# An attention kernel whose TensorE order is planned when it is built: a new order rule, GpSimd for part of the shifted exp terms, and up to 22 of 64 blocks for VectorE

## Chip, cores, metric

One core of one Trainium2 chip. The metric is the device time of the kernel in microseconds, the median of several executions. The program uses one core only, so an execution counts as slow when it is over 1.5% above the fastest of the same kernel; comparisons use the others.

## The reference

Two independent attention problems (the code is shortened here) over 2048 tokens, width 512, 32 heads of 16. B is plain full attention. A is causal attention inside four segments of 512 tokens, mixed with a linear-attention memory that is carried from segment to segment.

```python
def _B_ref(x, wqkv, wo):
    qkv = (x @ wqkv).reshape(B, S, 3, H, Dh).transpose(2, 0, 3, 1, 4)
    q, k, v = qkv[0], qkv[1], qkv[2]
    scores = jnp.einsum('bhqd,bhkd->bhqk', q, k) * Dh ** (-0.5)
    p = _softmax(scores, axis=-1)
    o = jnp.einsum('bhqk,bhkd->bhqd', p, v)
    return o.transpose(0, 2, 1, 3).reshape(B, S, D) @ wo

def _A_ref(x, wq, wk, wv, wo, beta):          # cut to its core, for each segment s
    a_dot = softmax(causal(qs @ ks.T * scale)) @ vs
    a_mem = (phi(qs) @ M) / (phi(qs) @ z + 1e-6)
    o = g * a_mem + (1 - g) * a_dot           # g = sigmoid(beta)
    M += phi(ks).T @ vs;  z += phi(ks).sum()
```

The time is in the exponentials: B alone has 32 x 2048 x 2048 of them.

## The kernel before

The unit of work in B is one pair of (chunk of 512 queries, group of 4 heads): 4 heads x 16 key blocks = 64 blocks of 128 keys x 512 queries. For each block TensorE makes the scores in PSUM, one engine makes the exp, and TensorE multiplies it with the values (called PV below) into one accumulator.

Most blocks get their exp from ScalarE, two or three blocks in one instruction. VectorE takes up to 19 of the 64. Its blocks use no exp instruction but the bits of float16. Score times a constant plus a bias, rounded to int16 and read as float16, is a rough power of two. Three such terms, shifted by 0, 341 and 682 and weighted with three constants, make a good exp. The weights sit in copies of the values (VD, made by GpSimd). So a VectorE block costs one eviction from PSUM, two adds in SBUF (made for two blocks at once) and three PV matmuls instead of one.

```python
EXP_D = (0.0, 341.0, 682.0)                       # the shifts
EXP_C = (1.921875 / 16, 1.5234375 / 16, 1.2109375 / 16)   # the weights, in VD
...
E1 = [(13, 0), (14, 1), (15, 2)]                  # 16 + 3 blocks may go to VectorE
...
def dve_adds():                                   # the pair evicted before the last block
    if pd_open["add"] is not None:
        tile, n, ready, ents = pd_open["add"]
        pd_open["add"] = None
        for k in range(1, NT):
            nc.vector.tensor_scalar(tile[:, k, 0:n, :], tile[:, 0, 0:n, :], EXP_D[k], None, ALU.add)
            dve_do(dve_cost(512 * n, 0.32), ready + 120)
            for e in ents[k]:
                e["ready"] = c["dve"] + LAT
...
def dve_bank(u, j=None):                          # one block on VectorE
    ...                                           # score matmul into a d_ps bank (two of these)
    nc.vector.tensor_scalar(pd[:, 0, n, :], bank[:], EXP_B, 0.0, ALU.add, ALU.max)
    d_done(dve_do(dve_cost(512), c["t"] + LAT))
    dve_adds()
```

All instructions stand in an order fixed at build time. The program keeps clocks of what it believes each engine does (`c["t"]` for TensorE, `c["act"]`, `c["dve"]`, `c["gp"]`), with assumed costs, and a loop picks the next thing for TensorE: a tile of scores for ScalarE if its PSUM slot is free, else a batch of PV matmuls, a projection, a block for VectorE, or a zero matmul (a "filler") that is meant to keep TensorE's clock up. TensorE is given its matmuls in this order. If an operand comes later than the plan believed, the matmuls behind it are held up too: the timeline after the result shows a case, a wait of 1.47 us.

```python
MM, DR, LAT = 218.0, 125.0, 250.0
def dve_cost(n, rate=1.09): return 75.0 + rate * n
def gp_do(n, ready, rate=1.05):
    c["gp"] = max(c["gp"], ready) + 100.0 + rate * n
    return c["gp"]
...
# in the loop, after a tile of scores for ScalarE has been tried (cut):
if (rd and (even >= 3 or done or (full and len(rd) >= 4) or (blocked and max(len(x) for x in byj) > 0))
        and (u["acc"] is not None or acc_free[0] <= t + 100) and (act_soon is None or act_soon > t + 200)):
    flush(u, 16 if done else min(even, 4) if even >= 3 else 3)       # a batch of PV matmuls
    continue
```

Of the kernel before, what the change touches and what calls it, by code (L numbers as in the profile page):

```python
# [35 lines left out]
NT = 3  # L36
# [5 lines left out]
def fast_path(ctx, tc, nc, A_x, A_wq, A_wk, A_wv, A_wo, A_beta, B_x, B_wqkv, B_wo, out, flag):  # L42
# [139 lines left out]

    E1 = [(13, 0), (14, 1), (15, 2)]
    useq = [("a", 0, hg) for hg in range(HG)]
# [45 lines left out]
    def d_done(time):  # L230
        dbank[dcount[0] % DBANKS] = time
        dcount[0] += 1
# [8 lines left out]
    def pe(ns, mode, key=None):  # L241

        if c["mode"] != mode or ses["base"] + max(ses["acc"].values(), default=0) < c["t"] - 1:
            if c["mode"] != mode:
                c["t"] += DR
            c["mode"] = mode
            ses["base"], ses["acc"] = c["t"], {}
        ses["acc"][key] = ses["acc"].get(key, 0.0) + ns
        c["t"] = max(c["t"], ses["base"] + ses["acc"][key])
        work.append((c["t"], ns / MM * 512 * {"full": 1.0, "col": 0.3, "row": 0.2}[mode]))  # L250

# [345 lines left out]
    def make_vd(u):  # L597
# [11 lines left out]
        second = VP_b[:, E1[0][0], o + 2 * VW * E1[0][1]:o + 2 * VW * E1[0][1] + VW]  # L609
        second = bass.AP(second.tensor, second.offset, [rows, [step, len(E1)], [1, VW]])  # L610
        for k in range(NT):
            mul = lambda dst, src: nc.gpsimd.tensor_scalar(dst, src, EXP_C[k], 1.0, ALU.mult, ALU.mult)  # L612
            mul(t[:, k, 0:NSB * VW].rearrange("p (i r w) -> p i r w", i=4, r=4), heads_of(0, [[4 * ROW, 4], [step, 4]]))
            mul(t[:, k, NSB * VW:(NSB + len(E1)) * VW].rearrange("p (r w) -> p r w", w=VW), second)
        nc.gpsimd.memset(t[:, :, NSL * VW:], 1.0)
        for k in range(NT):
            gp_do(288, max(v_ready.values()))
            gp_do(100, 0)
        VD_t[u["i"]] = t
# [38 lines left out]
    def act_tile_a(u):  # L658
# [16 lines left out]
        else:  # L675
            n = sum(512 - P * kbl for _, parts in banks for kbl, _ in parts)
            nc.scalar.activation(pT[:].rearrange("p b n -> p (b n)")[:, 0:n],  # L677
                                 pt[:].rearrange("p b n -> p (b n)")[:, 0:n], ACT.Exp, scale=0.25)
        sfree[sl] = act_do(act_cost(n), c["t"] + LAT)

        b = 0
        while b < len(banks):
            e = b + 1
            while e < len(banks) and (banks[e][1][0][0] == 3) == (banks[b][1][0][0] == 3):
# [4 lines left out]
                                    pattern=[[0, e - b], [0, w // P], [1, P]], channel_multiplier=-1)  # L689
            gp_do((e - b) * w, sfree[sl] + LAT)  # L690
            b = e
# [31 lines left out]
    def act_tile_b(u, n, but=None):  # L723
# [10 lines left out]
        nc.scalar.activation(pT[:, 0:n, :], pt[:, 0:n, :], ACT.Exp, scale=1.0 / (LOG2E * 1024.0))  # L734
        sfree[sl] = act_do(act_cost(512 * n), c["t"] + LAT)
        cnt = dict(n=n, kind=pt_out[sl])
        pt_out[sl][0] += 1
        for b, (kb, j) in enumerate(banks):
            h = 8 * u["rt"] + 2 * j + u["par"]
            u["pvq"].append(dict(j=j, c0=0, lhsT=VP_b[:, kb, VW * h:VW * h + 32], rhs=pT[:, b, :],  # L740
                                 ready=sfree[sl] + LAT, cnt=cnt, v=("b", kb)))
        return [j for _, j in banks]

    pd_open = dict(tile=None, n=0, add=None)

    def dve_adds():

        if pd_open["add"] is not None:
            tile, n, ready, ents = pd_open["add"]
            pd_open["add"] = None  # L750
            for k in range(1, NT):
                nc.vector.tensor_scalar(tile[:, k, 0:n, :], tile[:, 0, 0:n, :], EXP_D[k], None, ALU.add)  # L752
                dve_do(dve_cost(512 * n, 0.32), ready + 120)
                for e in ents[k]:
                    e["ready"] = c["dve"] + LAT

# [104 lines left out]
    def by_head(u, t):  # L861
        rd = pv_ready(u, t)
        return [[e for e in rd if e["j"] == j] for j in range(4)]

    def flush(u, rounds):

# [4 lines left out]
        for r in range(rounds):  # L871
            for j in range(4):
# [10 lines left out]
                if e["cnt"]["n"] == 0:  # L883
                    e["cnt"]["kind"][0] -= 1


# [21 lines left out]
    c.update(act=t0 + 700, dve=t0 + 1400)  # L908
    sfree[0] = sfree[1] = t0 + 900
    for u in U[:2]:  # L910
        u["ready"] = t0 + 300
# [6 lines left out]
    def fill_idle(until):  # L918
# [3 lines left out]
        n = 0  # L922
        while until - c["t"] > 300 and n < 8 and busy(until - 3413) < 3100:
            if u["acc"] is None:
# [23 lines left out]
    while True:  # L948
# [69 lines left out]
        if act_now is not None:  # L1018
# [12 lines left out]
            continue  # L1031

        u = U[pvi[0]]
        byj = by_head(u, t)
# [3 lines left out]
        even = min(len(x) for x in byj)  # L1038
        if (rd and (even >= 3 or done or (full and len(rd) >= 4) or (blocked and max(len(x) for x in byj) > 0))
                and (u["acc"] is not None or acc_free[0] <= t + 100) and (act_soon is None or act_soon > t + 200)):  # L1040
            flush(u, 16 if done else min(even, 4) if even >= 3 else 3)
            continue
        if due or du is not None or ch is not None:
            if dwhen <= t + 60:
                if due or (du is None and ch is not None and ch["due"] - 20000 <= prog[0]):
                    if act_soon is None or act_soon > t + 300:
                        chores.remove(ch)
                        ch["fn"]()
                        continue
                elif du is not None and (act_soon is None or act_soon > t + 400):  # L1050
                    dve_bank(du)
# [19 lines left out]
        fill_idle(nxt)  # L1071
        c["t"] = max(c["t"], nxt)
    run_later(1e18)
# [428 lines left out]
```

## Time and profile before

| | before |
|---|---|
| median of 4 executions | 972.54 us |
| ScalarE busy | 864.9 us (89%) |
| VectorE busy | 753.5 us (77%) |
| TensorE busy (matmuls overlap) | 822.3 us (84%) |
| GpSimd busy | 373.0 us (38%) |
| ScalarE idle (span less busy) | 111.7 us |

The profiled execution before had a span of 976.6 us; busy and idle times in this document are those of the profiled execution, times and ratios those of all.

The page of the kernel before. Its first line is busy time and instruction count by engine, PEclk is TensorE's granted clock in tenths over 40 slices of the span, the line with shares is the chain of work that ended last, and the lines with L numbers are groups: busy us, mean ns of one, then idle of that engine just before them and who ended it. In the names, s_ps and d_ps are scores for ScalarE and for VectorE, pT and pD their exps (pD holds the three shifted terms), acc is the PV accumulator.

```profile
PE 822.3 (84%) x6974; PEld 255.7 (26%) x6974; DVE 753.5 (77%) x1502; ACT 864.9 (89%) x803; POOL 373.0 (38%) x768
...
PEclk9999999898998999899999999999989998989977
...
PE 32%; ACT 28%; DVE 16%; issue 14%; POOL 9%; DMA 1%; ACTq 0%; DVEq 0%; POOLq 0%
...
L734 ACT ACTIVATE pT<-s_ps 128x1536 bf16<-128x1536 f32 (+2 forms) x613 | 701.5, 1253 | 68.8 <-PE d_ps L775 38.0
L786 DVE TENSOR_SCALAR pD<-d_ps 128x512 int16<-128x512 f32 x534 | 350.1, 680 | 56.6 <-PE d_ps L775 54.4
...
L877 PE MATMUL acc<-pD,VD 128*32 128x512 f16 x1602 | 240.5, 409 | 4.2 <-DVE tT L815 4.0
L752 DVE TENSOR_SCALAR pD<-pD 128x1024 int16<-128x1024 int16 (+1 forms) x538 | 234.1, 477 | 0.3
```

ScalarE is the busiest engine, and it idles 68.8 us before its B exps. 613 exps of 1253 ns on average are 768 us, but they are busy for 701.5 us only: one starts before the one ahead has ended. The PV matmuls on VectorE's terms hardly wait (4.2 us).

Who waited for whom, of the kernel before: the engine and its line, whom it waited for, us in total, times, the longest.

```profile
ACT pT L734 <- PE d_ps L775: 38.0, 48, 3.3
ACT pT L734 <- PE s_ps L729: 26.5, 32, 6.8
...
PE d_ps L775 <- DVE pD L786: 13.0, 30, 1.1
```

ScalarE waits for score matmuls (s_ps its own, d_ps those for VectorE that were issued beside them). TensorE waits little for VectorE to free a score bank.

Two stretches of 100 us of the kernel before: busy us and count by engine (PE, PEld, DVE, ACT, POOL), then the granted clock (the last two numbers are DMA).

```profile
500.00:600.00 100.00, 86.80 (x780) 26.48 (x779) 87.48 (x178) 95.21 (x88) 32.19 (x67) 0.97 0.02 7
800.00:900.00 100.00, 82.90 (x738) 25.26 (x738) 83.01 (x168) 90.53 (x83) 34.27 (x67) 0.91 0.00 1
```

ScalarE is above 90% in both, VectorE and TensorE not far below. The chain of waits has no single owner.

### The profile page before, as it was taken

To read this page: it belongs to the slowest core of one execution; us is meant where nothing else is said; L and a number is where in the kernel's file an instruction comes from. 1 tells how busy PE (TensorE), PEld (TensorE's weight loads), DVE (VectorE), ACT (ScalarE), POOL (GpSimd) and SP (SyncE) were. 2 spreads that over 40 slices of the span, in tenths; PEclk is the share of its full clock that TensorE was granted. 3 is DMA by queue.
4 is the path that set the end of the run, shared out by engine and by line. 5 is a ranking of instruction groups with operands and counts; after the bars stand their busy time and mean duration, and the time that the engine had idled before them with its cause. 6 is when DMAs were issued, how large, how long until landed. Compare 5 with 4: busy or idle time off the path is not lost.

```text
span 976.6 us, 18041 instructions
## 1 busy us (share of the span) xinstructions
PE 822.3 (84%) x6974; PEld 255.7 (26%) x6974; DVE 753.5 (77%) x1502; ACT 864.9 (89%) x803; POOL 373.0 (38%) x768
## 2 busy tenths in 40 slices
PE   5999998888888888898888898788988878888784
PEld 2333232222222222232222222222322222222221
DVE  3454668787888788869888987987478987989774
ACT  3898979898998889899999998989999998989982
POOL 3850625233333443444443154326345421514320
PEclk9999999898998999899999999999989998989977
DMA  7011000000000000010000000000000000000001
GB/s 221 23 44 39 6 22 2 1 1 2 1 2 12 12 1 1 6 34 1 1 1 18 6 1 1 1 1 3 22 1 12 12 1 2 1 1 1 1 7 42
DMA packets 14719, 13.83 MB, mean 14 GB/s; under 512 B 2336, under 2 KB 14624, under 8 KB 14624
## 3 DMA queue, kind: packets, MB, share of 16 engines
q1 hardware_dynamic: 12864, 11.54, 3.7%
q8 instruction: 56, 0.92, 0.4%
q10 hardware_dynamic: 1632, 1.05, 0.4%
q14 instruction: 39, 0.32, 0.1%
q0 software_dynamic: 128, 0.00, 0.0%
HBM read 8.39 MB, written 4.19 MB: 13 GB/s over the span
## 4 chain that ended last, share of the span: by engine, by line
PE 32%; ACT 28%; DVE 16%; issue 14%; POOL 9%; DMA 1%; ACTq 0%; DVEq 0%; POOLq 0%
ACT pT L734 23%; PE acc L877 13%; PE s_ps L729 8%; DVE pD L786 7%; DVE pD L752 5%; ACT pT L677 4%; POOL VD L612 4%; PE d_ps L324 3%; POOL pT L688 2%; PE d_ps L327 2%; DVE tT L815 2%; PE d_ps L494 2%; PE d_ps L775 1%; PE s_ps L667 1%; DMA beta_t<-in_A_beta_dram 1%
## 5 line engine op out<-in xcount | busy, mean ns | idle before, releaser
L734 ACT ACTIVATE pT<-s_ps 128x1536 bf16<-128x1536 f32 (+2 forms) x613 | 701.5, 1253 | 68.8 <-PE d_ps L775 38.0
L786 DVE TENSOR_SCALAR pD<-d_ps 128x512 int16<-128x512 f32 x534 | 350.1, 680 | 56.6 <-PE d_ps L775 54.4
L729 PE MATMUL s_ps<-QT_b,KT_b 32*128 32x512 bf16 x1514 | 242.1, 398 | 70.2 <-ACT pT L734 62.9
L877 PE MATMUL acc<-pT,VP_b 128*32 128x512 bf16 x1514 | 268.1, 409 | 0.0
L877 PE MATMUL acc<-pD,VD 128*32 128x512 f16 x1602 | 240.5, 409 | 4.2 <-DVE tT L815 4.0
L752 DVE TENSOR_SCALAR pD<-pD 128x1024 int16<-128x1024 int16 (+1 forms) x538 | 234.1, 477 | 0.3
L688 POOL TENSOR_SCALAR_AFFINE_SELECT pT<-pT 128x512 bf16<-128x512 bf16 (+3 forms) x192 | 97.7, 525 | 288.2 <-ACT pT L677 287.9
L775 PE MATMUL d_ps<-QT_b,KT_b 32*128 32x512 bf16 x534 | 186.4, 396 | 15.1 <-DVE pD L786 13.0
L729 PEld LDWEIGHTS <-KT_b 32*128 32x128 bf16 x1514 | 70.2, 91 | 295.3 <-issue 288.9
L677 ACT ACTIVATE pT<-s_ps 128x1024 bf16<-128x1024 f32 (+1 forms) x128 | 136.7, 1169 | 10.9 <-PE s_ps L667 9.4
L877 PEld LDWEIGHTS <-VP_b 128*32 128x32 bf16 x1514 | 68.5, 98 | 76.0 <-issue 54.4
L877 PEld LDWEIGHTS <-VD 128*32 128x32 bf16 x1602 | 59.5, 98 | 96.0 <-issue 83.1
L667 PE MATMUL s_ps<-QT_a,KT_a 32*128 32x384 bf16 (+3 forms) x512 | 57.7, 303 | 24.2 <-ACT pT L677 12.2
L612 POOL TENSOR_SCALAR VD<-VP_b 128x288 bf16<-128x288 bf16 (+1 forms) x186 | 66.9, 360 | 12.2
L815 DVE STREAM_TRANSPOSE tT<-acc 128x512 f32<-128x512 f32 x64 | 45.5, 711 | 31.4 <-PE acc L877 30.7
L877 PE MATMUL acc<-pT,VP_a 128*32 128x384 bf16 (+3 forms) x512 | 49.0, 318 | 16.2 <-POOL pT L688 12.8
L836 POOL TENSOR_TENSOR tN<-tT,RA 128x256 bf16<-128x256 f32 x31 | 20.1, 650 | 77.5 <-DVE RA L818 77.4
L337 POOL TENSOR_SCALAR QT_b<-qc,mq 128x512 bf16<-128x512 bf16 x32 | 24.1, 763 | 66.2 <-DVE qc L395 66.0
L775 PEld LDWEIGHTS <-KT_b 32*128 32x128 bf16 x534 | 40.1, 91 | 9.0 <-issue 7.7
L667 PEld LDWEIGHTS <-KT_a 32*128 32x128 bf16 x512 | 20.4, 92 | 79.5 <-issue 69.2
L337 POOL TENSOR_SCALAR QT_a<-qc,mq 128x512 bf16<-128x512 bf16 x30 | 21.8, 736 | 35.6 <-DVE qc L393 35.4
L504 DVE CAST osb<-d_ps 128x512 bf16<-128x512 f32 x28 | 19.1, 685 | 12.7 <-PE d_ps L494 12.7
(109 smaller groups left out, 613.9 us busy)
## 6 DMA issues: line engine op xcount, KB each, us to landing
out_dram<-osb SPq DMA_DIRECT2D x30, 128.0 KB, 1.7
xin<-in_B_x_dram SPq DMA_DIRECT2D x16, 128.0 KB, 2.2
xin<-in_A_x_dram SPq DMA_DIRECT2D x14, 128.0 KB, 2.1
wv_a<-in_A_wv_dram SPq DMA_DIRECT2D x1, 512.0 KB, 10.4
wv_b<-in_B_wqkv_dram SPq DMA_DIRECT2D x1, 512.0 KB, 9.9
wk_b<-in_B_wqkv_dram SPq DMA_DIRECT2D x1, 512.0 KB, 9.6
wq_b<-in_B_wqkv_dram SPq DMA_DIRECT2D x1, 512.0 KB, 10.0
wo_a<-in_A_wo_dram SPq DMA_DIRECT2D x1, 512.0 KB, 9.4
```

Of the source, the lines that this page charges most:

```text
L337: nc.gpsimd.tensor_scalar(t[:, par, :], qc[:], mq[:, par:par + 1], 1.0, ALU.mult, ALU.mult)
L612: mul = lambda dst, src: nc.gpsimd.tensor_scalar(dst, src, EXP_C[k], 1.0, ALU.mult, ALU.mult)
L667: nc.tensor.matmul(pt[:, b, col:col + w], kt[32 * j:32 * j + 32, kbl * P:(kbl + 1) * P], q[32 * j:32 * j + 32, P * kbl:512], start=(r == 0 ...
L677: nc.scalar.activation(pT[:].rearrange("p b n -> p (b n)")[:, 0:n], pt[:].rearrange("p b n -> p (b n)")[:, 0:n], ACT.Exp, scale=0.25)
L688: nc.gpsimd.affine_select(out=blk, in_=blk, compare_op=ALU.is_ge, fill=0.0, base=0, pattern=[[0, e - b], [0, w // P], [1, P]], channel_mul ...
L729: nc.tensor.matmul(pt[:, b, :], KT_b[32 * j:32 * j + 32, u["rt"], kb * P:(kb + 1) * P], q[32 * j:32 * j + 32, :], start=True, stop=True, t ...
L734: nc.scalar.activation(pT[:, 0:n, :], pt[:, 0:n, :], ACT.Exp, scale=1.0 / (LOG2E * 1024.0))
L752: nc.vector.tensor_scalar(tile[:, k, 0:n, :], tile[:, 0, 0:n, :], EXP_D[k], None, ALU.add)
L775: nc.tensor.matmul(bank[:], KT_b[32 * j:32 * j + 32, u["rt"], kb * P:(kb + 1) * P], qslice(u)[32 * j:32 * j + 32, :], start=True, stop=Tru ...
L786: nc.vector.tensor_scalar(pd[:, 0, n, :], bank[:], EXP_B, 0.0, ALU.add, ALU.max)
L815: nc.vector.transpose(tT[:].rearrange("p c d -> p (c d)"), u["acc"][:])
L877: nc.tensor.matmul(u["acc"][32 * j:32 * j + 32, e["c0"]:512], e["lhsT"], e["rhs"], start=(j not in u["started"]), stop=False, tile_positio ...
```

## The change

Its intent: ScalarE limits, so give VectorE more blocks (16 + 6 of 64). To make room on VectorE, give GpSimd, 38% busy, the second add of a pair when the plan says that GpSimd is free. And cut what TensorE does between two tiles of scores to what fits into the work that ScalarE still has queued (`room`), with smaller PV batches and more fillers against a falling clock. The core of the diff (cut: the layout of VD for six extra blocks, some latencies, the same test for projections):

```diff
-    E1 = [(13, 0), (14, 1), (15, 2)]
+    E1 = [(9, 0), (10, 1), (11, 2), (13, 0), (14, 1), (15, 2)]
...
+    GPS = -500
...
             for k in range(1, NT):
-                nc.vector.tensor_scalar(tile[:, k, 0:n, :], tile[:, 0, 0:n, :], EXP_D[k], None, ALU.add)
-                dve_do(dve_cost(512 * n, 0.32), ready + 120)
+                gp = k == NT - 1 and n == 2 and c["gp"] < c["dve"] + GPS
+                (nc.gpsimd if gp else nc.vector).tensor_scalar(tile[:, k, 0:n, :], tile[:, 0, 0:n, :], EXP_D[k], None, ALU.add)
+                if gp:
+                    gp_do(512 * n, ready + LAT)
+                else:
+                    dve_do(dve_cost(512 * n, 0.32), ready + 120)
...
+        if len(u["started"]) == 4 and busy(c["t"] - 3213) < WARM2:     # in flush: fillers
+            for j in range(4):
+                nc.tensor.matmul(u["acc"][32 * j:32 * j + 32, :], zero[:, 0:32], wq_a[:, 0, :], ...)
...
+        room = 1e9
+        if au is not None and not blocked and not stalled:
+            room = max(c["act"] - LATE, act_soon or 0) - t + SLK
...
-        if (rd and (even >= 3 or done or (full and len(rd) >= 4) or ...
-            flush(u, 16 if done else min(even, 4) if even >= 3 else 3)
-            continue
+        if rd and (u["acc"] is not None or acc_free[0] <= t + 100):
+            want = most if done else even if even >= EVEN else min(3, most) if full and (len(rd) >= 4 or blocked) else 0
+            r = int(min(want, 4 if not done else 16, (room - DR) // MM))
+            if r > 0 and (r >= min(want, 2) or blocked):
+                flush(u, r)
+                continue
```

More of the change, by code (lines that the diff above doesn't have):

```diff
@@ L230, in d_done @@
     def d_done(time):
-        dbank[dcount[0] % DBANKS] = time
+        dbank[dcount[0] % DBANKS] = time + 100
         dcount[0] += 1
@@ L249, in pe @@
         c["t"] = max(c["t"], ses["base"] + ses["acc"][key])
-        work.append((c["t"], ns / MM * 512 * {"full": 1.0, "col": 0.3, "row": 0.2}[mode]))
+        work.append((c["t"], ns / MM * 512 * {"full": 1.0, "col": 0.35, "row": 0.2}[mode]))
     def act_cost(n):
@@ L609, in make_vd @@
         second = VP_b[:, E1[0][0], o + 2 * VW * E1[0][1]:o + 2 * VW * E1[0][1] + VW]
-        second = bass.AP(second.tensor, second.offset, [rows, [step, len(E1)], [1, VW]])
+        second = bass.AP(second.tensor, second.offset, [rows, [4 * ROW, 2], [step, 3], [1, VW]])
         for k in range(NT):
@@ L613, in make_vd @@
             mul(t[:, k, 0:NSB * VW].rearrange("p (i r w) -> p i r w", i=4, r=4), heads_of(0, [[4 * ROW, 4], [step, 4]]))
-            mul(t[:, k, NSB * VW:(NSB + len(E1)) * VW].rearrange("p (r w) -> p r w", w=VW), second)
+            mul(t[:, k, NSB * VW:(NSB + len(E1)) * VW].rearrange("p (i r w) -> p i r w", i=2, w=VW), second)
         nc.gpsimd.memset(t[:, :, NSL * VW:], 1.0)
@@ L617, in make_vd @@
             gp_do(288, max(v_ready.values()))
-            gp_do(100, 0)
+            gp_do(150, 0)
         VD_t[u["i"]] = t
@@ L678, in act_tile_a @@
                                  pt[:].rearrange("p b n -> p (b n)")[:, 0:n], ACT.Exp, scale=0.25)
-        sfree[sl] = act_do(act_cost(n), c["t"] + LAT)
+        sfree[sl] = act_do(act_cost(n), c["t"] + LAT) + 100
         b = 0
@@ L689, in act_tile_a @@
                                     pattern=[[0, e - b], [0, w // P], [1, P]], channel_multiplier=-1)
-            gp_do((e - b) * w, sfree[sl] + LAT)
+            gp_do((e - b) * w, sfree[sl] + 100)
             b = e
@@ L734, in act_tile_b @@
         nc.scalar.activation(pT[:, 0:n, :], pt[:, 0:n, :], ACT.Exp, scale=1.0 / (LOG2E * 1024.0))
-        sfree[sl] = act_do(act_cost(512 * n), c["t"] + LAT)
+        sfree[sl] = act_do(act_cost(512 * n), c["t"] + LAT) + 100
         cnt = dict(n=n, kind=pt_out[sl])
@@ L740, in act_tile_b @@
             u["pvq"].append(dict(j=j, c0=0, lhsT=VP_b[:, kb, VW * h:VW * h + 32], rhs=pT[:, b, :],
-                                 ready=sfree[sl] + LAT, cnt=cnt, v=("b", kb)))
+                                 ready=sfree[sl] + 100, cnt=cnt, v=("b", kb)))
         return [j for _, j in banks]
     pd_open = dict(tile=None, n=0, add=None)
+    GPS = -500
     def dve_adds():
@@ L751, in dve_adds @@
             for k in range(1, NT):
-                nc.vector.tensor_scalar(tile[:, k, 0:n, :], tile[:, 0, 0:n, :], EXP_D[k], None, ALU.add)
-                dve_do(dve_cost(512 * n, 0.32), ready + 120)
+                gp = k == NT - 1 and n == 2 and c["gp"] < c["dve"] + GPS
[4 more added lines that the diff above has]
+                    dve_do(dve_cost(512 * n, 0.32), ready + 120)
                 for e in ents[k]:
-                    e["ready"] = c["dve"] + LAT
+                    e["ready"] = c["gp" if gp else "dve"] + LAT
     def has_keys(u, kb):
@@ L863, in by_head @@
         return [[e for e in rd if e["j"] == j] for j in range(4)]
+    GAP, WARM, WARM2 = 200, 3300, 2900
     def flush(u, rounds):
@@ L884, in flush @@
                     e["cnt"]["kind"][0] -= 1
+        if len(u["started"]) == 4 and busy(c["t"] - 3213) < WARM2:
+            for j in range(4):
+                nc.tensor.matmul(u["acc"][32 * j:32 * j + 32, :], zero[:, 0:32], wq_a[:, 0, :], start=False, stop=False,
+                                 tile_position=(0, 32 * j), skip_group_check=True)
+                pe(MM, "col", j)
     vdn = [0]
@@ L909, in fast_path @@
     sfree[0] = sfree[1] = t0 + 900
+    LATE, SLK, EVEN = 470.0, 400.0, 2
     for u in U[:2]:
@@ L922, in fill_idle @@
         n = 0
-        while until - c["t"] > 300 and n < 8 and busy(until - 3413) < 3100:
+        while until - c["t"] > GAP and n < 8 and busy(until - 3413) < WARM:
             if u["acc"] is None:
@@ L1038, in fast_path @@
         even = min(len(x) for x in byj)
-        if (rd and (even >= 3 or done or (full and len(rd) >= 4) or (blocked and max(len(x) for x in byj) > 0))
-                and (u["acc"] is not None or acc_free[0] <= t + 100) and (act_soon is None or act_soon > t + 200)):
-            flush(u, 16 if done else min(even, 4) if even >= 3 else 3)
-            continue
+        most = max(len(x) for x in byj)
+        if rd and (u["acc"] is not None or acc_free[0] <= t + 100):
[4 more added lines that the diff above has]
+                continue
         if due or du is not None or ch is not None:
@@ L1045, in fast_path @@
                 if due or (du is None and ch is not None and ch["due"] - 20000 <= prog[0]):
-                    if act_soon is None or act_soon > t + 300:
+                    if room >= 4 * MM + DR:
                         chores.remove(ch)
@@ L1049, in fast_path @@
                         continue
-                elif du is not None and (act_soon is None or act_soon > t + 400):
+                elif du is not None and room >= MM + DR:
                     dve_bank(du)
@@ L1071, in fast_path @@
         fill_idle(nxt)
-        c["t"] = max(c["t"], nxt)
+        c["t"] = max(c["t"], min(nxt, t + 300))
     run_later(1e18)
```

## The prediction

> **What bounds it now.** ScalarE. The page's busy table: ScalarE 864.9 us (89%), VectorE 753.5 (77%), TensorE 822.3 (84%, overlapping matmuls), GpSimd 373.0 (38%). In the chain of waits the exps of B tiles lead with 23%. By the stretches view ScalarE's 112 us of idle are about 37 us at the start (to 25 us) and end (from 950), and 74 us in the body. The groups view puts most of these behind late score matmuls: 38.0 us behind VectorE blocks' scores, 26.5 behind its own. By the clock and instruction records TensorE ran at half clock for 102 us of the body, in windows of 3.4 or 6.8 us, and 36 of ScalarE's 74 idle us lie in them, 11% of the time. So two causes of similar size: too much work between score tiles, and half-clock windows that double it. The Trainium skill, "TensorE: Matmul & The Clock Gate", Part 1, says that the clock halves after an idle window of about 3.4 us; the records show such windows.
>
> **What changes (instruction order of both builds, times of the trace).**
> - Blocks to VectorE: 534 becomes 590. ScalarE's exps of 1536 fall from 299 to 271, of 1024 rise from 303 to 315, of 512 from 11 to 15: at 1478, 1053, 642 ns that is 26 us less, about 839.
> - VectorE: +56 evictions at 680 ns (+38 us); 190 second adds go to GpSimd, and its long adds fall from 530 to 398 (-63 us at 480 ns).
> - GpSimd: +190 adds of 1024 elements. Its 54-, 288- and 512-element forms (272, 448, 690 to 760 ns) extrapolate to 1.1 to 1.2 us (estimate): +215 us, about 600.
> - Contention: VectorE adds begun while GpSimd was busy took 639 ns on average, others 416. The Trainium skill, "SBUF — State Buffer", Who interferes with whom, names a shared port pair held by one of the two at a time; the trace agrees. With GpSimd 60% busy I estimate VectorE's adds at 550 to 650 ns, which eats most of the 63 us. VectorE ends near 770 us: not relieved, no bound.
> - TensorE: 112 more PV matmuls (4 abreast, 6 us), 125 warm-up matmuls instead of 26 (8 us), more switches between small batches.
> - Order: flushes, projections and VectorE scores are cut to the room that ScalarE's queue leaves.
>
> **On the critical path.** ScalarE's 26 us count in full. Of the 74 us of body idle I expect 50 to remain: half-clock time from 102 us to about 60 and shorter batches, offset by less slack on TensorE and VectorE. 839 + 37 + 50 = 926.
>
> **Predicted: 926 us, range 902 to 954. Faster by over 2%: 0.88; within 2%: 0.10; slower: 0.02.**
>
> **What would show it.** ScalarE busy 835 to 843, body idle 35 to 65; granted clock up from 0.94 to 0.95 or more; GpSimd 570 to 640, each moved add 1.0 to 1.3 us; VectorE adds over 530 ns, VectorE 755 to 785; ScalarE's idle behind VectorE blocks' scores under 25 us.
>
> **What would make it wrong.** GpSimd and VectorE adds blocking each other more than estimated: score banks come free late, TensorE waits in order, ScalarE starves (up to 955). Half-clock windows not falling, since smaller batches leave gaps. Or the fit works nearly fully, body idle near 25 us (about 900).

## The result, and the profile after

| | before | after |
|---|---|---|
| median of 4 executions | 972.54 us | 1155.49 us |
| ScalarE busy / idle | 864.9 / 111.7 us | 859.8 / 288.2 us |
| VectorE busy | 753.5 us | 812.2 us |
| GpSimd busy | 373.0 us | 919.1 us |
| mean granted clock | 0.940 | 0.865 |

The kernel is slower, with a ratio of 1.188 (95% interval 1.180 to 1.195). Ratios here are the mean time of one kernel's fast runs over that of the other's of the same rounds, so not quite the ratio of the medians quoted. All later ratios are to the kernel before in the same rounds.

The page of the kernel after, the same lines and the new one:

```profile
PE 939.9 (82%) x7132; PEld 260.1 (23%) x7185; DVE 812.2 (71%) x1422; ACT 859.8 (75%) x791; POOL 919.1 (80%) x958
...
PEclk9999988987889889968787878799978868789887
...
POOL 40%; PE 28%; DVE 14%; issue 9%; ACT 6%; DMA 1%; DVEq 0%; ACTq 0%; POOLq 0%
...
L734 ACT ACTIVATE pT<-s_ps 128x1536 bf16<-128x1536 f32 (+2 forms) x601 | 690.4, 1211 | 199.6 <-PE d_ps L781 121.8
L755 POOL TENSOR_SCALAR pD<-pD 128x1024 int16<-128x1024 int16 x190 | 542.2, 2877 | 38.8 <-DVE pD L792 38.8
...
L885 PE MATMUL acc<-pD,VD 128*32 128x512 f16 x1770 | 310.3, 446 | 111.0 <-POOL pD L755 106.9
...
L755 DVE TENSOR_SCALAR pD<-pD 128x1024 int16<-128x1024 int16 (+1 forms) x402 | 254.6, 655 | 0.5
```

The second of the L lines is the finding. One GpSimd add takes 2877 ns; VectorE needed about 480 for the same, and the plan assumed 1175. 190 of them are 542 us. The chain of waits has moved to GpSimd (40%). The PV matmuls on VectorE's terms, which waited 4.2 us before, wait 111 us, nearly all for that add. ScalarE's idle before its B exps has grown from 68.8 to 199.6 us.

The waits of the kernel after, those shown of before and the new one:

```profile
ACT pT L734 <- PE d_ps L781: 121.8, 113, 3.4
PE acc L885 <- POOL pD L755: 106.9, 114, 2.5
ACT pT L734 <- PE s_ps L729: 66.2, 74, 4.8
...
PE d_ps L781 <- DVE pD L792: 23.3, 53, 1.4
```

And two stretches of the kernel after:

```profile
500.00:600.00 100.00, 84.86 (x607) 20.70 (x610) 69.63 (x119) 72.80 (x66) 90.80 (x83) 0.77 0.02 5
900.00:1000.00 100.00, 82.29 (x585) 19.43 (x581) 69.27 (x121) 68.80 (x63) 89.25 (x74) 0.77 0.00 1
```

GpSimd is the busiest engine there, ScalarE has fallen to about 70%, and the clock to 0.77: TensorE waits for GpSimd, then also runs slower. The clock records give 313 us at half clock, against 118 before. A TensorE that still counts as busy for 85 us of 100 did 607 matmuls where it did 780.

A few lines of the timeline of the kernel after (start, duration in us; in brackets the engine's idle before and its releaser):

```profile
498.22 0.39 PE L885 MATMUL acc<-pD,VD 128*32 128x512 f16 x1
498.72 0.42 DVE L755 TENSOR_SCALAR pD<-pD 128x1024 int16<-128x1024 int16 x1
499.05 0.68 DVE L792 TENSOR_SCALAR pD<-d_ps 128x512 int16<-128x512 f32 x1
500.07 0.58 PE L885 MATMUL acc<-pD,VD 128*32 128x512 f16 x1 [1.47 <-POOL pD L755]
...
501.05 0.61 PE L729 MATMUL s_ps<-QT_b,KT_b 32*128 32x512 bf16 x2
...
501.76 1.02 ACT L734 ACTIVATE pT<-s_ps 128x1024 bf16<-128x1024 f32 x1 [1.33 <-PE d_ps L781]
501.80 0.69 DVE L792 TENSOR_SCALAR pD<-d_ps 128x512 int16<-128x512 f32 x1 [2.07 <-PE d_ps L781]
```

TensorE stands still for 1.47 us until GpSimd's add is done. The scores behind that matmul start at 501.05 only, and they run at half clock (0.61 us instead of 0.39). ScalarE and VectorE idle 1.33 and 2.07 us. The page names the score matmuls as those who kept ScalarE waiting, and one has to go one step further to see what kept the score matmuls.

### The profile page after: what moved, and what is told of

Read it like the earlier page. It is cut to its first block, busy times and chain, and to the rows that moved or that the text cites. A ratio compares the mean times of both kernels' runs of the same rounds, so it can differ in the third digit from the quotient of the medians.

```text
span 1148.0 us, 18786 instructions
## 1 busy us (share of the span) xinstructions
PE 939.9 (82%) x7132; PEld 260.1 (23%) x7185; DVE 812.2 (71%) x1422; ACT 859.8 (75%) x791; POOL 919.1 (80%) x958
## 3 DMA queue, kind: packets, MB, share of 16 engines
q10 hardware_dynamic: 1632, 1.05, 0.3%
## 4 chain that ended last, share of the span: by engine, by line
POOL 40%; PE 28%; DVE 14%; issue 9%; ACT 6%; DMA 1%; DVEq 0%; ACTq 0%; POOLq 0%
POOL pD L755 30%; PE acc L885 12%; DVE pD L792 6%; PE s_ps L729 5%; ACT pT L734 4%; DVE pD L755 4%; PE d_ps L324 3%; POOL VD L612 3%; PE s_ps L667 2%; PE d_ps L327 2%; PE d_ps L781 2%; POOL pT L688 2%; ACT pT L677 1%; DVE tT L821 1%; PE d_ps L494 1%
## 5 line engine op out<-in xcount | busy, mean ns | idle before, releaser
L734 ACT ACTIVATE pT<-s_ps 128x1536 bf16<-128x1536 f32 (+2 forms) x601 | 690.4, 1211 | 199.6 <-PE d_ps L781 121.8
L755 POOL TENSOR_SCALAR pD<-pD 128x1024 int16<-128x1024 int16 x190 | 542.2, 2877 | 38.8 <-DVE pD L792 38.8
L792 DVE TENSOR_SCALAR pD<-d_ps 128x512 int16<-128x512 f32 x590 | 391.0, 678 | 159.6 <-PE d_ps L781 132.8
L885 PE MATMUL acc<-pD,VD 128*32 128x512 f16 x1770 | 310.3, 446 | 111.0 <-POOL pD L755 106.9
L885 PE MATMUL acc<-pT,VP_b 128*32 128x512 bf16 x1458 | 314.2, 434 | 0.3 <-issue 0.3
L729 PE MATMUL s_ps<-QT_b,KT_b 32*128 32x512 bf16 x1458 | 258.1, 424 | 19.9 <-ACT pT L734 14.5
L755 DVE TENSOR_SCALAR pD<-pD 128x1024 int16<-128x1024 int16 (+1 forms) x402 | 254.6, 655 | 0.5
L781 PE MATMUL d_ps<-QT_b,KT_b 32*128 32x512 bf16 x590 | 214.0, 429 | 27.0 <-DVE pD L792 23.3
L667 PE MATMUL s_ps<-QT_a,KT_a 32*128 32x128 bf16 (+3 forms) x512 | 67.1, 343 | 4.8 <-ACT pT L677 2.5
L885 PE MATMUL acc<-pT,VP_a 128*32 128x512 bf16 (+3 forms) x512 | 48.6, 338 | 12.0 <-POOL pT L688 5.5
```

The source lines that it names most:

```text
L667: nc.tensor.matmul(pt[:, b, col:col + w], kt[32 * j:32 * j + 32, kbl * P:(kbl + 1) * P], q[32 * j:32 * j + 32, P * kbl:512], start=(r == 0 ...
L729: nc.tensor.matmul(pt[:, b, :], KT_b[32 * j:32 * j + 32, u["rt"], kb * P:(kb + 1) * P], q[32 * j:32 * j + 32, :], start=True, stop=True, t ...
L734: nc.scalar.activation(pT[:, 0:n, :], pt[:, 0:n, :], ACT.Exp, scale=1.0 / (LOG2E * 1024.0))
L755: (nc.gpsimd if gp else nc.vector).tensor_scalar(tile[:, k, 0:n, :], tile[:, 0, 0:n, :], EXP_D[k], None, ALU.add)
L781: nc.tensor.matmul(bank[:], KT_b[32 * j:32 * j + 32, u["rt"], kb * P:(kb + 1) * P], qslice(u)[32 * j:32 * j + 32, :], start=True, stop=Tru ...
L885: nc.tensor.matmul(u["acc"][32 * j:32 * j + 32, e["c0"]:512], e["lhsT"], e["rhs"], start=(j not in u["started"]), stop=False, tile_positio ...
```

## Experiments

The theory after reading: the slow GpSimd add, through TensorE's fixed order, is the loss. Its rivals: the new order rule or the larger share of blocks is bad by itself; or GpSimd and VectorE block each other. Kernels named "chained" and so on are explained where they first appear. All results below were correct.

### 1. No adds on GpSimd

```diff
-                gp = k == NT - 1 and n == 2 and c["gp"] < c["dve"] + GPS
+                gp = False
```

> The changed kernel with every shifted add left on VectorE; all else of the change stays (22 blocks, the fit to ScalarE's queue, the new fillers), and the build's order follows (557 blocks on VectorE, 590 before). Theory (the 190 adds on GpSimd at 2.88 us each are the loss: the PV matmuls wait for them in order, TensorE cools, the scores come late): ScalarE busy near 856 us, granted clock back to 0.93 or more, time 925 to 960 us. Rival (the new order with small batches, or the larger share of blocks, is itself bad): still over 1050 us.

Measured: 964.74 us, ratio 0.991 (0.985 to 0.997), granted clock 0.959, ScalarE 857.0 us busy and 106.7 idle. The loss is gone, so the adds on GpSimd carry it. But the time is just above the range expected: the rest of the change, without them, is worth about 1%, not 5%.

### 2. GpSimd adds alone, in the kernel before

The same rule for the second add, added to the kernel before; no other part of the change.

> The kernel before with the GpSimd adds alone (same rule for which adds go, 185 go; 19 blocks, old order rules, old fillers). Theory: the adds alone do the harm, so 185 adds at about 2.9 us, granted clock under 0.90, time 1080 to 1180 us. Rival (the harm needs the new order or the 22 blocks): 965 to 1000 us.

Measured (one execution, so its state is unknown): 1131.62 us. 185 adds at 2885 ns, half-clock time 289 us, PV matmuls 102.0 us behind the adds. The adds alone do nearly all of the harm; they don't need the new order.

### 3. Another form of the add

The quick GpSimd scalar instructions of the trace before all have two operations, the slow add has one.

```diff
-  nc.gpsimd.tensor_scalar(out, in, EXP_D[k], None, ALU.add)
+  nc.gpsimd.tensor_scalar(out, in, EXP_D[k], 0.0, ALU.add, ALU.add)
```

> The changed kernel in exactly its order, with only the form of the GpSimd add altered: add c, then add 0, in place of a single add. Every quick GpSimd scalar instruction of the trace before has two operations; the slow add has one. Theory A (the one-operation form is what is slow): each moved add falls to 1.1 to 1.3 us, GpSimd busy to about 600 us, time 915 to 955 us. Rival B (int16 operands are slow on GpSimd in either form): still about 2.9 us each and about 1155 us. Rival C (they are slow because VectorE holds the port): also still slow, with a wide spread.

Measured: 1319.24 us, ratio 1.354 (1.348 to 1.361). The guess was wrong, and the other way: 3699 ns for each add. The run is useful all the same. With every engine's order unchanged, an add that is 0.82 us longer costs another 164 us; the PV matmuls' wait for it went from 106.9 to 192.8 us and half-clock time to 634 us. VectorE was busy less than in the kernel after (777.9 against 812.2 us). A group and a wait of this run:

```profile
L756 POOL TENSOR_SCALAR pD<-pD 128x1024 int16<-128x1024 int16 x190 | 698.5, 3699 | 38.1 <-DVE pD L795 37.9
...
PE acc L888 <- POOL pD L756: 192.8, 156, 3.2
```

So it is the wait for the late term, not VectorE being blocked, that scales with the loss.

### 4. GpSimd by itself: which forms are slow

A row of GpSimd instructions at the end of the kernel before, when GpSimd has nothing else to do.

> The kernel before with a row of GpSimd instructions at its end, when GpSimd has no other work: 1024 elements of int16 and of bf16, add, mult and max, each in the one-operation and in the two-operation form, and int16 at 512. If the form is the cause: one-operation about 2.8 us, two-operation 1.1 to 1.2 us, in int16 and in bf16 alike. If int16 is the cause: int16 slow in both forms, bf16 quick in both. If contention is the cause: all near 1.1 us here. The time itself (about 60 us longer) is of no interest.

The groups of this run on GpSimd. L1087 is int16 plus c, L1088 plus c plus 0, L1093 bf16 times c, L1094 bf16 times c times 1, L1096 bf16 plus c, L1097 bf16 plus c plus 0.

```profile
L1088 POOL TENSOR_SCALAR probe<-probe 128x1024 int16<-128x1024 int16 x3 | 11.0, 3657 | 0.3
L1097 POOL TENSOR_SCALAR probe<-probe 128x1024 bf16<-128x1024 bf16 x3 | 10.9, 3640 | 0.2
...
L1087 POOL TENSOR_SCALAR probe<-probe 128x1024 int16<-128x1024 int16 x3 | 8.4, 2797 | 0.3
L1093 POOL TENSOR_SCALAR probe<-probe 128x1024 bf16<-128x1024 bf16 x3 | 8.3, 2777 | 0.2
L1096 POOL TENSOR_SCALAR probe<-probe 128x1024 bf16<-128x1024 bf16 x3 | 8.3, 2773 | 0.2
...
L1094 POOL TENSOR_SCALAR probe<-probe 128x1024 bf16<-128x1024 bf16 x3 | 3.1, 1046 | 0.2
```

Neither int16 nor contention is the cause: the add is as slow in bf16 and with GpSimd otherwise idle. All three expectations missed the pattern: one operation costs 2.8 us in every case tried (plus, times, max), two cost 3.65 us, and one pair, times then times, costs 1.05 us. That pair is just what the kernel's masks and weights used.

### 5. Which pairs are quick

> The kernel before with a second row of GpSimd instructions at its end, 1024 int16 elements each, two of each: mult then add, add then mult, add then min, add then max, subtract then add, mult then mult, min then max, an int32 tensor-tensor add over the same bytes (512 elements), and a copy. Theory (a few pairs of operations have a quick routine, all else a slow general one): mult-mult and min-max at about 1.05 us in int16 too, and perhaps mult-add; the rest near 3.6 us. Rival (int16 has no quick routine at all): everything 2.8 us or more. The int32 add: about 1.2 us, from the 512-element tensor-tensor adds of the trace before.

The timeline of GpSimd at the end of this run, two of each, all int16 of 1024 but the int32. L1086 is times then plus, L1088 plus then times, L1090 plus then min, L1098 min then max, L1100 the int32 add of two tensors.

```profile
953.60 2.17 POOL L1086 TENSOR_SCALAR probe<-probe 128x1024 int16<-128x1024 int16 x2
955.85 2.17 POOL L1088 TENSOR_SCALAR probe<-probe 128x1024 int16<-128x1024 int16 x2
958.11 7.72 POOL L1090 TENSOR_SCALAR probe<-probe 128x1024 int16<-128x1024 int16 x2
...
983.03 2.16 POOL L1098 TENSOR_SCALAR probe<-probe 128x1024 int16<-128x1024 int16 x2
985.28 2.60 POOL L1100 TENSOR_TENSOR probe<-probe 128x512 int32<-128x512 int32 x2
```

Half of 2.17 us is 1.085 us each: times-plus, plus-times, times-times and min-max are quick, in int16 too; plus-min, plus-max and minus-plus took 3.7 to 3.9 us each. The int32 add took 1.30 us and a copy 1.07. So the add can be had at about 1.09 us by writing it as times 1.0, plus c.

### 6. The changed kernel with the quick form

```diff
-  nc.gpsimd.tensor_scalar(out, in, EXP_D[k], None, ALU.add)
+  nc.gpsimd.tensor_scalar(out, in, 1.0, EXP_D[k], ALU.mult, ALU.add)
```

> The changed kernel, every engine's order unchanged; only the GpSimd add is written as times 1.0, then plus c, which took 1085 ns by itself in the probe (plus then plus: 3.66 us, plus alone: 2.8 us). Theory (the duration of that one instruction is the whole of the failure): each moved add 1.1 to 1.3 us, GpSimd about 600 us, time 915 to 950 us, that is, my prediction holds once its wrong term is mended. Rival (my body-idle term was wrong as well, as the small gains of the runs without GpSimd adds hint): 955 to 975 us, with ScalarE busy near 839 us and its body idle still over 75 us.

Measured: 1010.76 us, ratio 1.035 (1.029 to 1.041). Both expectations missed. The form took away 145 of the 183 us lost, but the kernel is still slower than before, though the add is as quick as the prediction had assumed (1058 ns). The groups of this run on VectorE and GpSimd that made the shifted terms, with both shapes apart:

```profile
L758 DVE TENSOR_SCALAR pD<-pD 128x1024 int16<-128x1024 int16 x398 | 268.9, 696 | 0.5
...
L756 POOL TENSOR_SCALAR pD<-pD 128x1024 int16<-128x1024 int16 x190 | 201.0, 1058 | 193.4 <-DVE pD L795 193.0
```

The same group in the kernel before:

```profile
L752 DVE TENSOR_SCALAR pD<-pD 128x1024 int16<-128x1024 int16 x530 | 232.2, 480 | 0.3
```

VectorE does 398 long adds instead of 530 but is busy with them for 269 us instead of 232. Its timeline shows why:

```profile
203.26 1.05 POOL L756 TENSOR_SCALAR pD<-pD 128x1024 int16<-128x1024 int16 x1 [0.84 <-DVE pD L795]
203.66 0.93 DVE L758 TENSOR_SCALAR pD<-pD 128x1024 int16<-128x1024 int16 x1
...
205.94 1.05 POOL L756 TENSOR_SCALAR pD<-pD 128x1024 int16<-128x1024 int16 x1 [1.62 <-DVE pD L795]
206.41 0.85 DVE L758 TENSOR_SCALAR pD<-pD 128x1024 int16<-128x1024 int16 x1
```

Both adds of a pair need the same thing, the evicted pair, so they mostly start within half a microsecond of each other (150 of 173 that overlap), and VectorE's add mostly ends after GpSimd's (161 of them). By the instruction records, 173 VectorE adds overlapped a GpSimd add by over 50 ns and took 857 ns on average; those that met no GpSimd work took 407. The Trainium skill, "SBUF — State Buffer", section "Who interferes with whom", says that VectorE in a two-port mode and GpSimd exclude each other for a whole instruction; that is what these numbers look like. Each add given away saves about 480 ns and costs the add beside it about 450. VectorE is late with its next evictions, score banks come free late (TensorE waits 54.7 us for them, 13.0 before), and ScalarE waits behind.

### 7. The quick adds alone, in the kernel before

> The kernel before with 185 GpSimd adds in the times-then-plus form, nothing else of the change (the one-operation form of the same took 1131.6 us). Theory: 940 to 970 us, since VectorE gets 11 more blocks and has fewer adds. Rival (GpSimd adds harm also when quick, by blocking VectorE): over 980 us.

Measured: 1006.95 us, ratio 1.031 (1.024 to 1.038). The rival was right. 185 quick adds on GpSimd make the untouched kernel 3% slower; 167 VectorE adds overlap one of them, at 853 ns. It doesn't need a saturated VectorE: it was busy 764.3 us of 1008.

### 8. The slow add, with its true cost in the plan

```diff
-                    gp_do(512 * n, ready + LAT)
+                    gp_do(512 * n, ready + LAT, 2.71)
```

> The changed kernel with its slow add kept, but with the scheduler told the add's true cost (2.88 us in place of 1.18): 102 adds then go to GpSimd instead of 190, 560 blocks to VectorE, and PV matmuls are placed when the results are due. If the harm comes from an order planned for results that come 1.7 us later than planned: 950 to 985 us, with PV matmuls waiting for GpSimd under 20 us (107 in the changed kernel). If a 2.9 us add is harmful in itself (VectorE blocked while it runs, GpSimd's other work held up): 1040 to 1090 us, about half of the loss for half of the adds.

Measured: 1008.28 us, ratio 1.035 (1.029 to 1.040), between the two expectations. The waits of this run list no PV matmul behind a GpSimd add any more, so that part of the first theory held: an order that knows of the 2.9 us adds is rid of the wait. This plan also moves only 102 adds, with 560 blocks on VectorE, so the fall of the loss is not due to the order alone. What remains looks like section 6, though no run parts it here: the VectorE adds that overlapped a GpSimd add took 683 ns.

### 9. No overlap inside a pair ("chained")

GpSimd takes the first shifted term, which VectorE makes, and adds the difference of the shifts. The value is the same, but it can only start when VectorE's add is done. Every engine's order is that of the kernel after.

```diff
-  nc.gpsimd.tensor_scalar(tile[:, k, 0:n, :], tile[:, 0, 0:n, :], 1.0, EXP_D[k], ALU.mult, ALU.add)
+  nc.gpsimd.tensor_scalar(tile[:, k, 0:n, :], tile[:, k - 1, 0:n, :], 1.0, EXP_D[k] - EXP_D[k - 1], ALU.mult, ALU.add)
```

> The changed kernel in its own order, quick GpSimd add as before, with one operand altered: the GpSimd add takes the first shifted term (made by VectorE) and adds the difference, instead of taking the unshifted term. The value is the same, but it can start only when VectorE's own add of the pair is done, so the two no longer run at the same time (173 VectorE adds overlapped a GpSimd add and took 857 ns on average; adds that met no GpSimd work took 407). Theory (the rest of the loss is VectorE's adds blocked by the GpSimd add of the same pair): overlapped adds under 60, VectorE's adds at 430 to 520 ns on average, VectorE busy 715 to 750 us, time 925 to 960 us. Rival (the rest of the loss is the order itself, or the later second term): 990 us or more though VectorE is no longer blocked.

Measured: 980.05 us, ratio 1.004 (0.998 to 1.011). The groups:

```profile
L756 POOL TENSOR_SCALAR pD<-pD 128x1024 int16<-128x1024 int16 x190 | 199.1, 1048 | 200.1 <-DVE pD L758 108.0 <-PE d_ps L784 61.1 <-PE acc L888 26.8
L758 DVE TENSOR_SCALAR pD<-pD 128x1024 int16<-128x1024 int16 x398 | 195.1, 512 | 0.5
```

The mechanism is as stated: overlaps fell from 173 to 68 (under 60 was expected) and those took 476 ns, VectorE's long adds fell from 269 to 195 us, VectorE's busy time from 815 to 750 us, and 3% of time came back. The time, however, is above the forecast of 925 to 960: ScalarE is busy 848.1 us, 17 less than in the kernel before, and idle 134.0 us, 22 more.

The same alteration in the kernel before with GpSimd adds alone:

> The same alteration in the kernel before with 185 quick GpSimd adds (1007 us while the two overlapped). Theory: VectorE busy 690 to 720 us, time 940 to 965 us, under the 974 of the kernel before. Rival: 990 us or more.

Measured: 980.44 us, ratio 1.007 (1.003 to 1.011), against 1.031 of section 7 in the same order: the step shows in a second order too. VectorE was 701.3 us busy, 52 us less than in the kernel before. In this build, whose order differs from that of the kernel before, 7% less busy time on VectorE did not make the kernel faster.

### 10. The order rule alone, and the blocks alone

The changed kernel without GpSimd adds and with 19 blocks:

> The changed kernel without GpSimd adds and with the old 19 blocks: the fit to ScalarE's queue and the fillers alone. 540 blocks fall to VectorE (534 before), ScalarE busy about 861 us. If the small gain of the run without GpSimd adds (0.9%) came from the fit: 960 to 970 us with the granted clock near 0.96. If it came from the blocks: 970 to 980 us.

Measured: 971.27 us over all four runs, one of them slow (965.85 over the fast ones), ratio of fast runs 0.994 (0.985 to 1.003); its profile fell into the slow run and is not used. No change that can be told from zero.

The kernel before with `E1` of six instead of three, and nothing else:

> The kernel before with up to 22 blocks for VectorE and nothing else. The build takes only 537 (534 before), in other tiles: 282 exps of 1536, 326 of 1024, 13 of 512. ScalarE busy about 865 us as before. If blocks need VectorE's time more than permission: 970 to 985 us, the same as before. If permission was what lacked: under 965 us.

Measured: 961.06 us over all four runs, one of them slow (958.09 over the fast ones), ratio of fast runs 0.984 (0.977 to 0.992). VectorE got 3 blocks more (537), in other tiles; ScalarE's work is nearly the same (1511 blocks in 621 exps, 1514 in 613 before). So 1.6% came with a mere rearrangement, against the first expectation. What in it helps is not shown.

### 11. Is TensorE's load what ate the gain?

TensorE's work has grown: 112 more PV matmuls and 99 more fillers, by count. First, more TensorE work in the kernel before, order and plan unchanged: four zero matmuls abreast after each fourth PV batch, not told to the plan.

> The kernel before in its own order and plan, with four zero matmuls abreast added after each fourth PV batch: 119 sets of about 0.22 us, some 26 us of TensorE work; results unchanged. If TensorE limits together with ScalarE: the time rises by 10 to 26 us (984 to 1000), ScalarE busy unchanged and its idle larger; a rise of the granted clock may take some of it back. If TensorE has slack between the score tiles: within 5 us of the kernel before, or faster by the clock.

Measured: 980.15 us, ratio 1.003 (0.999 to 1.007). About 26 us of work (estimate, 119 times 0.22 us) cost nothing that can be told from zero. Half-clock time was 79 us in the profile, against 118 in that of the kernel before, and the granted clock was 0.956 to 0.964 in its runs against 0.941 to 0.951.

Then the chained kernel with its fillers not issued:

> The chained kernel (980 us) in its own order and plan, with 122 of its 125 zero matmuls not issued: about 13 us of TensorE work less. If TensorE's load is what ate the gain: 965 to 975 us. If the fillers earn their time by the clock: granted clock under 0.93 and 985 us or more.

Measured: 989.18 us, ratio 1.010 (1.006 to 1.015), granted clock 0.922, half-clock time 156 us against 104 with fillers. Without fillers the clock fell in every run (0.922 to 0.929; with fillers, in other rounds, 0.943 to 0.961), as the second expectation said; the time is longer too, but its interval and that of the chained kernel (0.998 to 1.011) overlap. Of the load that fillers make, then, no cost is seen; that of the 112 PV matmuls was not tested by itself. The Trainium skill, "TensorE: Matmul & The Clock Gate", Part 1, describes a clock that halves when the array was idle for a window; both runs agree in direction. "Idle" doesn't fit this trace to the letter: in the body of the kernel before, the 21 full-clock windows of 3.4 us that were followed by half clock were 46 to 83% busy on TensorE (65% on average, the other full-clock windows 87%).

### 12. A plan with true costs

The planner of both kernels compared takes 0.63 us for an eviction and 0.40 us for a VectorE add of a pair. The chained kernel with measured costs instead: 0.68 us for an eviction, 0.51 us for a VectorE add (its mean with blocking), 1.05 us for a GpSimd add that starts after it.

```diff
-    def dve_cost(n, rate=1.09):
+    def dve_cost(n, rate=1.18):
...
-                    gp_do(512 * n, ready + LAT)
+                    gp_do(512 * n, c["dve"] + LAT, 0.925)
-                    dve_do(dve_cost(512 * n, 0.32), ready + 120)
+                    dve_do(dve_cost(512 * n, 0.42), ready + 120)
```

> The chained kernel with the scheduler told what was measured: eviction 0.68 us, VectorE add 0.51 us, GpSimd add 1.05 us and only after VectorE's add. 557 blocks and 170 GpSimd adds. If a plan with wrong costs is what ate the gain: 945 to 965 us, ScalarE's body idle under 70 us. If not: 970 to 985 us.

Measured: 960.33 us, ratio 0.981 (0.977 to 0.985), within the first expectation for the time. ScalarE 857.3 us busy and 109.6 idle, of which 76 us between 25 and 950 us, where under 70 was expected. But the profile is of the slowest of five runs (968.67 us, clock 0.957; the others had 958.34 to 961.62 us and 0.972 to 0.974). If ScalarE's work took as long in those, their idle was 7 to 10 us less (estimate), so that part of the expectation stays open. The page's first line of this run and its chain of waits:

```profile
PE 855.1 (88%) x7135; PEld 261.8 (27%) x7135; DVE 732.8 (76%) x1375; ACT 857.3 (89%) x806; POOL 552.3 (57%) x938
...
PE 42%; ACT 26%; issue 10%; DVE 10%; POOL 9%; DMA 1%; ACTq 0%; DVEq 0%; POOLq 0%
```

GpSimd is down to 9% of the chain, VectorE to 10%. With this the changed kernel is faster than both of the kernels compared, though against the kernel before by no margin that is clear of 2%. The true plan gives VectorE fewer blocks, 557, than the false one, 590, and is faster with them.

### 13. What the gain needs

The true-plan kernel without GpSimd adds:

> The true-plan kernel without GpSimd adds: 533 blocks on VectorE (557 with them), ScalarE busy about 867 us (857 with them). If the GpSimd adds are worth their 24 blocks: 967 to 978 us, about 10 us above the true-plan kernel. If they are worth nothing: 957 to 966 us.

Measured: 969.62 us, ratio 0.996 (0.991 to 1.000), within the first expectation. ScalarE 866.9 us busy and 99.9 idle, the least idle of all runs profiled.

True costs, chained adds and 22 blocks, but the old order rules and fillers:

> True costs, chained quick GpSimd adds (152) and up to 22 blocks (531 go), but the old order rules and fillers. If true costs alone bring the gain: 955 to 965 us, as the true-plan kernel. If the new order rules are needed with it: 967 to 980 us, since without them only 531 blocks go to VectorE and ScalarE is busy about 867 us.

Measured: 975.07 us, ratio 1.000 (0.998 to 1.002), within the second expectation.

And the same with the old, too cheap costs:

> The kernel before with 22 blocks and chained quick GpSimd adds, but its own order rules and fillers: 562 blocks to VectorE, 178 adds on GpSimd, ScalarE about 852 us. If the new order rules are what costs: 945 to 960 us, the best of all. If GpSimd adds bring nothing (as in the kernel before, 980 us): 962 to 985 us, no better than the blocks alone (961 us).

Measured: 965.44 us, ratio 0.989 (0.984 to 0.995), within the second expectation.

With true costs, taking out either the GpSimd adds or the new rules costs 1.4 to 1.9% (0.996 and 1.000 against 0.981). But the last pair shows that true costs are not better in every setting: under the old rules the cheap costs were 1% faster. Differences of 1 to 2% between builds come with the arrangement itself, and the runs don't say by which rule.

## Why the prediction was wrong

The prediction was 926 us with a range to 954; it measured 1155.5. That ScalarE is the busiest engine before was read from the trace and stands. That what it saves counts in full does not: in the chained kernel it was busy 17 us less, and the kernel was no faster. Then, point by point:

- **"1.1 to 1.2 us (estimate)" for the GpSimd add: this is the step that failed.** It measured 2.88 us. The estimate went from the size of other GpSimd instructions to this one, as if only the element count mattered. The scalar ones among those were times-times and min-max, the quick pairs; the add had one operation. 190 adds at 2.88 us put GpSimd at 919 us, against "about 600". With only the form altered in an unchanged order, 1155 us became 1011. That is the largest part of the miss and not all of it: 1011 is still above 954, by the next point and the idle of ScalarE below.
- **"VectorE's adds at 550 to 650 ns": mechanism right, size off.** The trace before held the contention (639 ns against 416), and it was read as a chance of meeting GpSimd. But GpSimd's new add starts with VectorE's add of the same pair, so they meet by construction: 655 ns in the kernel after, 692 ns with the quick form, where GpSimd's busy time did come out near the forecast (580 us). Chaining the operands took 3% of time back, and its overlapped adds dropped from 857 to 476 ns.
- **"VectorE ends near 770 us: not relieved, no bound": half right.** 812 us. VectorE busy for 815 us of 1009 is no bound by its share, yet TensorE waited 54.7 us for its score banks, 13.0 before. The question is not whether an engine is full but whether it is late for something that waits in order.
- **"26 us less, about 839" for ScalarE: too much.** 848.1 us in the chained kernel, in the same tiles: 17 us less. The same 791 instructions in the same order were busy 848.1 to 863.5 us in the runs of this document, so busy time isn't a fixed sum. A likely part of the miss, not tested: means of overlapping instructions were multiplied by counts; 613 exps sum to 768 us by their means and are busy 701.5.
- **"Of the 74 us of body idle I expect 50 to remain": not reached in any profiled run.** (By the stretches view the body had 76 us before.) Total ScalarE idle was 111.7 us before, 106.7 without GpSimd adds, 134.0 chained, 109.6 with the true plan, 99.9 with the true plan and no GpSimd adds; the prediction had 87. Half-clock time did fall (118 us before, then 82, 104, 86 and 60), as expected, but the idle followed only in part. By the clock and instruction records, body idle (from 25 us to 27 us before the end) inside half-clock windows fell from 37 us to 20 with the true plan and 14 with it and no GpSimd adds, but outside them it rose from 39 to 53 and 47. So even the best version gained 2%, not 5%.
- **"Score banks come free late, TensorE waits in order, ScalarE starves (up to 955)": the right chain under the risks, with a bound that was far too small.** There was also a shorter way: TensorE waited for GpSimd's term itself, 107 us.

In ratios to the kernel before, the same order of instructions gives 1.188 with the slow form, 1.035 with the quick form and 1.004 when the two adds of a pair no longer meet. A rebuilt order with true costs gives 0.981. The first two steps are shown by single edits in an unchanged order. The third is one run against another build. Open is why the new order rule, which was to cut ScalarE's idle, hardly does, and why the mere permission for other blocks was worth 1.6%.

## What to carry to other kernels

Before moving an operation to another engine, measure that very instruction there, with its operations, type and size; a neighbour of another form can be off by a factor of 2.7. Then ask what starts at the same moment as the moved work: two engines that wait for the same result and block each other will meet again and again (here 173 VectorE adds met the 190 on GpSimd), and an operand taken one step later can part most of them (68 still met). Where the order is fixed at build time, a wrong cost in the plan can be paid by every engine behind the late one (the wait for the 2.88 us add), so correct the plan's costs before judging the idea, and measure again: correcting its smaller errors helped here under the new rules and not under the old.

## What the Trainium skill lacked or had wrong

- "GPSIMD Engine Reference", section 4.1 Engine selection, calls one-input elementwise work on GpSimd roughly line-rate. Here that holds for some forms only: 1024 elements took 1.05 to 1.09 us as times-times, times-plus, plus-times or min-max, 2.8 us as a single operation, and 3.6 to 3.9 us as any other pair tried, in int16 (plus-plus and the single add in bf16 alike). The page doesn't say that it matters which operations are paired.
- "SBUF — State Buffer", section "Who interferes with whom", has the loser of the shared port blocked for the whole instruction. With the quick add that fits: of 165 VectorE adds begun during one, none ended before it did. With the slow, 2.88 us form it does not: 104 VectorE adds began and ended inside one by the records (GpSimd's spans there are rough), half of them in 418 ns or less, so that form does not seem to hold the port throughout.
- "TensorE: Matmul & The Clock Gate", Part 1, says what to fear from an idle TensorE but gives no price for filling. Here 26 us of zero matmuls (estimate) in the kernel before cost no time that can be told from zero (ratio 1.003, 0.999 to 1.007), and leaving out 122 fillers in the chained kernel lowered the clock from 0.948 to 0.922 in the profiles, with ratios of 1.004 and 1.010 whose intervals overlap.
